# Threshold attention and a relu-squared MLP on one core: the first batch in two sweeps, MLP work in smaller pieces at an even rate, a float64 rounding in three VectorE passes, squares on GpSimd

## The chip, the core and the metric

The kernel runs on one core of a Trainium2 chip. A core has five engines that run side by side, each through its own queue in order: PE (TensorE, matrix products and transposes, results in PSUM), DVE (VectorE), ACT (ScalarE), POOL (GpSimd) and SP (SyncE, which here issues nearly all DMAs). PE loads a stationary operand (PEld in the profile) while it streams an earlier one. On this kernel an fp32 product shows as two matmul instructions, a transpose as one. The metric is the time of one execution on the device in microseconds, less being better.

## What is computed

Two blocks follow each other. The attention has 8 batches of 8 heads, 576 tokens, 64 columns a head:

```python
scores = scale * np.matmul(q, k.transpose(0, 1, 3, 2))          # scale = 1/8
thresh = np.max(scores, axis=-1, keepdims=True) - tau
scores = np.where(scores >= thresh, scores, -1000000000.0)
scores = scores - np.max(scores, axis=-1, keepdims=True)
attn = np.exp(scores)
attn = attn / (np.sum(attn, axis=-1, keepdims=True) + 1e-09)
return np.matmul(attn, v)
```

Its result, as x of 4608 tokens by 512 columns, goes through an MLP with 2048 hidden columns:

```python
h = x @ w_in
r = np.maximum(h, 0.0)
g = r * r
return g @ w_out
```

q, k and v are float32. w_in and w_out reach the kernel as float64, which it takes as pairs of 32-bit words and turns into float32 itself.

## The kernel before

**Attention steps.** Heads are taken in pairs, 4 pairs a batch, 32 in all. A pair has 5 steps: step `i` of 0 to 3 handles 128 query rows of both heads; step 4 handles the last 64 rows of both heads together, with `qmid`, in which the two heads' rows lie block by block. There are 160 steps `s`, 20 for a batch. `scores(g, i)` puts the scores into the PSUM tile `sc` (L167; one buffer of four banks), takes the row maximum on DVE (L172), small values beside it (L173 to L178), the exponential on ACT (L182), the threshold mask with the row sum on DVE (L183), a reciprocal (L186), and the normalisation on POOL (L188). The next `scores` waits until L183 has read `sc`.

`turn(g, i, part)` transposes those weights on PE one step later, in three parts of three 128x128 tiles (L200), each copied to `wT` by ACT (L201) out of one PSUM buffer, tag `tr`. `mix(g, half)` multiplies `wT` with `v` (L227) for 288 of a pair's 576 tokens, twice a pair, and ACT copies the result to `xT` (L230).

**MLP.** Tokens go in 12 chunks of 384. `mlp_in(j, f)` is one of 16 tiles of hidden columns: four products into `h` (L239), relu on ACT (L242), and on DVE the product of `h` and the relu, which is the square (L244). `mlp_out(j, x)` is a quarter of one 128-token output tile, four products (L255); after the fourth, a copy on ACT (L259) and a DMA (L261). Tiles `h` and `o` share two PSUM buffers, tag `mm`.

**Order.** PE runs the written order (`manual_schedule`). The queues of the other engines are ordered by the scheduler of the framework, which can put an instruction ahead of ones that were written earlier. `fill(share)` stands after each part of `turn` and at the end of a step and takes MLP work from a list: `add_chunks` adds the chunks whose tokens are complete, at step 1 of the first pair of the next batch, and `fill` spreads what is there over the rest of that batch. A batch has 576 tokens and a chunk 384, so batches 1 to 7 work on one chunk and two chunks in turn; two chunks remain after the last step.

**Loads.** `load_qk` loads q and k of a pair in 8 DMAs and is written two pairs ahead; `prep` transposes them in 32x32 blocks on DVE (L143), with small copies on POOL (L146, L150). `load_v` loads v in 4 DMAs into one of two tiles. `load_weights` and `round_weights` treat w_in and w_out in 32 pieces of 128x512, two pieces a step, over steps 0 to 17. The raw words lie in an area that is later the second `xT` buffer, with space for two pieces and their scratch. A piece passes DVE (L103), POOL (L104), ACT (L106), DVE (L107, L109, L110), POOL (L111) and DVE (L112).

Of the kernel before, what the change touches and what calls it, by code (L numbers as in the profile page):

```python
# [9 lines left out]
FP32 = mybir.dt.float32  # L10
# [7 lines left out]
def kernel(  # L18
# [66 lines left out]

    def weight_area(i):
        if not area:
            area["a"] = pool.tile([P, NMC, 2 * S], FP32, tag="xT", name="area").rearrange("p c s -> p (c s)")
        at = (i % 2) * 4 * WP
        return (area["a"][:, at:at + 2 * WP], area["a"][:, at + 2 * WP:at + 3 * WP],  # L90
                area["a"][:, at + 3 * WP:at + 4 * WP])

    def load_weights(i):
        nc.sync.dma_start(out=weight_area(i)[0].bitcast(mybir.dt.int64), in_=weight_piece(i)[0])

    def round_weights(i):


        src, p, f = weight_area(i)
        words = src.bitcast(U32).rearrange("p (n w) -> p n w", w=2)  # L100
        lo, hi = words[:, :, 0], words[:, :, 1]
        pu, fu, dst = p.bitcast(U32), f.bitcast(U32), weight_piece(i)[1]
        nc.vector.tensor_scalar(out=fu, in0=hi, scalar1=0x7FF00000, scalar2=None, op0=ALU.bitwise_and)  # L103
        nc.gpsimd.tensor_scalar(out=p, in0=fu, scalar1=float(1151 << 20), scalar2=float(896 << 20),  # L104
                                op0=ALU.min, op1=ALU.max)
        nc.scalar.activation(out=pu, in_=p, func=AF.Copy, bias=-float(896 << 23), scale=8.0)  # L106
        nc.vector.tensor_scalar(out=fu, in0=hi, scalar1=3, scalar2=0x007FFFFF,  # L107
                                op0=ALU.logical_shift_left, op1=ALU.bitwise_and)
        nc.vector.tensor_tensor(out=fu, in0=fu, in1=pu, op=ALU.bitwise_or)  # L109
        nc.vector.scalar_tensor_tensor(out=p, in0=lo, scalar=2.0 ** -52, in1=p, op0=ALU.mult, op1=ALU.mult)  # L110
        nc.gpsimd.tensor_tensor(out=f, in0=f, in1=p, op=ALU.add)  # L111
        nc.vector.scalar_tensor_tensor(out=dst.bitcast(U32), in0=hi, scalar=0x80000000, in1=fu,  # L112
                                       op0=ALU.bitwise_and, op1=ALU.bitwise_or)
# [3 lines left out]
    def load_qk(g):  # L117

        b, h = g // HP, 2 * (g % HP)
        tiles = []  # L120
        for name, t in (("ql", q), ("kl", k)):
            x = pool.tile([P, S // 32, 32], FP32, tag=name, name=name)
            for n in range(4):
                src = t[b, h + n // 2, :, (n % 2) * 32:(n % 2) * 32 + 32]
                nc.sync.dma_start(out=x[n * 32:(n + 1) * 32, :, :], in_=src.rearrange("(c p) d -> p c d", p=32))
            tiles.append(x)
        loaded[g] = tiles

    def load_v(g):
        b, h = g // HP, 2 * (g % HP)  # L130
        t = vs[g % 2]
        for u in range(2):
            at = u * (NBLK + 1)
            nc.sync.dma_start(out=t[:, at:at + NBLK, :],
                              in_=v[b, h + u, 0:NBLK * P, :].rearrange("(c p) d -> p c d", p=P))
            nc.sync.dma_start(out=t[u * D:(u + 1) * D, at + NBLK, :], in_=v[b, h + u, NBLK * P:S, :])

    def prep(g, part):

        if part == 0:  # L140
            ready[g] = [pool.tile([P, S], FP32, tag="qT", name="qT"), pool.tile([P, REST + S], FP32, tag="kT", name="kT")]
        qT, kT = ready[g]
        nc.vector.transpose((qT, kT[:, REST:])[part], loaded[g][part].rearrange("p c d -> p (c d)"))  # L143
        if part == 1:

            nc.gpsimd.tensor_copy(out=kT[D:P, 0:REST], in_=kT[D:P, S:S + REST])  # L146
        else:
            for u in range(2):
                rows = slice(u * D, (u + 1) * D)
                nc.gpsimd.tensor_copy(out=qmid[g % 2][rows, u * D:(u + 1) * D], in_=qT[rows, NBLK * P:S])  # L150
# [3 lines left out]
    def scores(g, i):  # L154


        qT, kT = ready[g]
        n = 2 if i < NBLK else 1
        sc = psum.tile([P, 2 * n, 512], FP32, tag="sc", name="sc")
        for half in range(2):  # L160
            for u in range(n):
                if i < NBLK:
                    rows, lhsT = slice(u * D, (u + 1) * D), qT[u * D:(u + 1) * D, i * P:(i + 1) * P]
                else:
                    rows, lhsT = slice(0, P), qmid[g % 2]
                at = (0 if u else REST) + half * HALF
                nc.tensor.matmul(sc[:, 2 * u + half, 0:HALF], lhsT, kT[rows, at:at + HALF],  # L167
                                 start=True, stop=True)
# [21 lines left out]
        weights[g, i] = w  # L190

    def turn(g, i, part):

        w = weights[g, i]
        ps = psum.tile([P, 4, P], FP32, tag="tr", name="w_ps")
# [21 lines left out]
    def mix(g, half):  # L217

        b, pr = g // HP, g % HP
        if b // 2 not in xTs:  # L220
            xTs[b // 2] = pool.tile([P, NMC, 2 * S], FP32, tag="xT", name="xT")
        cols = slice(half * HALF, (half + 1) * HALF)
        ps = psum.tile([P, HALF], FP32, tag="x", name="x_ps")
        for c in range(NBLK + 1):
            for u in range(2):
                cw = NBLK if c == NBLK else u * (NBLK + 1) + c
                nc.tensor.matmul(ps[u * D:(u + 1) * D, :], vs[g % 2][:, u * (NBLK + 1) + c, :], wT[:, cw, cols],  # L227
                                 start=(c == 0), stop=(c == NBLK))
        to = (b % 2) * S + half * HALF
        nc.scalar.copy(xTs[b // 2][:, pr, to:to + HALF], ps)  # L230
# [3 lines left out]
    def mlp_in(j, f):  # L234

        xT, at = xTs[j * TCH // (2 * S)], j * TCH % (2 * S)
        h = psum.tile([P, TCH], FP32, tag="mm", name="h", bufs=2)
        for c in range(NMC):
            nc.tensor.matmul(h, w_in_sb[:, c, f * P:(f + 1) * P], xT[:, c, at:at + TCH],  # L239
                             start=(c == 0), stop=(c == NMC - 1))  # L240
        r = pool.tile([P, TCH], FP32, tag="r", name="r")
        nc.scalar.activation(out=r, in_=h, func=AF.Relu)  # L242
        gs[j, f] = pool.tile([P, TCH], FP32, tag="g", name="g", bufs=17)
        nc.vector.tensor_tensor(out=gs[j, f], in0=h, in1=r, op=ALU.mult)  # L244

    OQ = 4

    def mlp_out(j, x):

        t, part = divmod(x, OQ)  # L250
# [3 lines left out]
        for f in range(part * NFT // OQ, (part + 1) * NFT // OQ):  # L254
            nc.tensor.matmul(o, gs[j, f][:, t * P:(t + 1) * P], w_out_sb[:, f, :],  # L255
                             start=(f == 0), stop=(f == NFT - 1))
        if part == OQ - 1:
# [5 lines left out]
    waiting = deque()  # L263
    state = {"chunk": 0, "left": 0.0}

    def add_chunks(tokens):
        while state["chunk"] < NCH and (state["chunk"] + 1) * TCH <= tokens:
            j = state["chunk"]
            waiting.extend((3.0, mlp_in, j, f) for f in range(NFT))
            waiting.extend((4.0, mlp_out, j, x) for x in range(TCH // P * OQ))  # L270
            state["chunk"] += 1

    def fill(share):


        total = sum(x[0] for x in waiting)
        state["left"] = min(state["left"] + (total / share if share else 1e9), total)
        while waiting and state["left"] >= waiting[0][0]:
            cost, fn, j, x = waiting.popleft()
            state["left"] -= cost  # L280
            fn(j, x)

    load_qk(0)
    load_v(0)
    load_qk(1)
    for part in range(2):
        prep(0, part)
    NST = NBLK + 1
    steps = [(g, i) for g in range(NPAIR) for i in range(NST)]
    per_batch = HP * NST  # L290
    for s in range(len(steps) + 2):
        g, i = divmod(s, NST)
        shares = 4 * (per_batch - s % per_batch)
        if s < len(steps):
            if i == 0 and 0 < g < NPAIR - 1:
                load_qk(g + 1)
            scores(g, i)
        if i == 1 and g > 0:
            mix(g - 1, 1)
            if g % HP == 0:  # L300
                add_chunks((g // HP) * S)
        for part in range(3):
            if 0 < s <= len(steps):
                turn(*steps[s - 1], part)
            fill(shares - part)
        if s < len(steps):
            if i == 4:
                mix(g, 0)
            if i == 2 and g + 1 < NPAIR:
                load_v(g + 1)  # L310
            if i in (2, 3) and g + 1 < NPAIR:
                prep(g + 1, i - 2)
            if s < n_pieces // 2 + 2:
                for x in (0, 1):
                    if s >= 1 and 2 * s - 2 + x < n_pieces:
                        round_weights(2 * s - 2 + x)
                    if 2 * s + x < n_pieces:
                        load_weights(2 * s + x)
        fill(shares - 3)
    fill(0)  # L320


# [30 lines left out]
```

## Time and profile before

| | us |
|---|---|
| median of 3 runs | 1853.54 |
| lowest and highest run | 1852.3, 1853.58 |
| the profiled execution | 1854.62 |
| its span, first to last instruction | 1852.9 |
| PE busy in the span | 1602.0 |
| DVE busy | 789.2 |
| ACT busy | 570.2 |
| POOL busy | 366.7 |
| mean granted PE clock | 0.95 |

A row of groups reads: line, engine, operation, output<-input, shapes, count, busy us in all and mean ns of one, then the idle time of the engine just before these instructions and what ended it. A row of the timeline reads: start, duration, engine, line, operation, and in brackets the idle time before it. A row by windows gives the stretch and its length, then the busy time of PE, PE's weight loads, DVE, ACT and POOL in it with counts, the granted PE clock as a share of full speed, the DMA share and GB/s. A row of waits gives who waited for whom, us in all, how often, and the longest.

### The profile page before, as it was taken

The numbers are of one execution on the slowest core, as the hardware profiler recorded it, in microseconds if no ns is written. First come the engines' busy times: TensorE is split into PE (matmuls) and PEld (weight loads), VectorE is DVE, ScalarE is ACT, GpSimd is POOL, SyncE is SP. The second block draws the span as 40 slices with busy tenths as digits, with TensorE's granted clock in tenths as the row PEclk, the third lists the DMA queues.
The fourth block names the chain that finished last, engine by engine and source line by source line (L and its number), as shares of the span: only waits on it lengthen the run. The fifth ranks groups of instructions, "written<-read, shape, count | busy, mean of one in ns | idle before, by whom it ended". The sixth has DMA issues, their size and how long they took to land.

```text
span 1852.9 us, 18593 instructions
## 1 busy us (share of the span) xinstructions
PE 1602.0 (86%) x6464; PEld 858.0 (46%) x6464; DVE 789.2 (43%) x1953; ACT 570.2 (31%) x1125; POOL 366.7 (20%) x619
## 2 busy tenths in 40 slices
PE   3455479888999989888999989898999989889999
PEld 2222245445555445445545445444545445445454
DVE  5767845444334345434334335434334335441010
ACT  2333233333323233333223234333223234332010
POOL 4555522111111112111111112221111111120000
PEclk9665589999999999999999999999999999999999
DMA  4433211110010111111011101111011010000000
GB/s 95 118 93 102 85 21 25 26 31 14 18 32 13 24 25 20 29 24 23 13 30 20 25 19 26 21 30 23 16 30 20 16 28 7 7 12 6 12 6 17
DMA packets 200382, 55.74 MB, mean 30 GB/s; under 512 B 191584, under 2 KB 191584, under 8 KB 200288
## 3 DMA queue, kind: packets, MB, share of 16 engines
q1 hardware_dynamic: 200256, 54.55, 13.0%
q8 instruction: 51, 0.84, 0.2%
q14 instruction: 43, 0.35, 0.1%
q0 software_dynamic: 32, 0.00, 0.0%
HBM read 45.09 MB, written 9.44 MB: 29 GB/s over the span
## 4 chain that ended last, share of the span: by engine, by line
PE 76%; DVE 9%; ACT 8%; POOL 4%; issue 3%; DMA 1%; SPq 0%; ACTq 0%; DVEq 0%; POOLq 0%
PE h L239 26%; PE o L255 24%; PE sc L167 9%; PE x_ps L227 9%; PE w_ps L200 8%; ACT w L182 3%; DVE w L183 3%; ACT wT L201 3%; POOL w L188 2%; POOL area L111 1%; DVE st L172 1%; DVE area L109 1%; POOL area L104 1%; PE w_ps L204 1%; DVE area L110 1%
## 5 line engine op out<-in xcount | busy, mean ns | idle before, releaser
L239 PE MATMUL h<-xT,w_in_sb 128*128 128x384 f32 x1536 | 520.9, 487 | 0.0
L255 PE MATMUL o<-w_out_sb,g 128*128 128x512 f32 x1152 | 514.8, 593 | 0.0
L239 PEld LDWEIGHTS h<-xT,w_in_sb 128*128 128x128 f32 x1536 | 280.6, 190 | 171.2 <-issue 6.7
L172 DVE TENSOR_REDUCE st<-sc 128x2 f32<-128x1152 f32 (+1 forms) x160 | 197.8, 1236 | 376.4 <-PE sc L167 372.9
L188 POOL TENSOR_SCALAR w<-w,st 128x576 f32<-128x576 f32 x288 | 242.8, 851 | 466.9 <-DVE st L186 445.4
L200 PE MATMUL w_ps<-ident,w 128*128 128x128 f32 x1152 | 216.6, 300 | 123.0 <-ACT wT L201 105.3
L183 DVE SCALAR_TENSOR_TENSOR w<-sc,st,w 128x576 f32<-128x576 f32 x288 | 235.4, 817 | 184.6 <-ACT w L182 183.0
L255 PEld LDWEIGHTS o<-w_out_sb,g 128*128 128x128 f32 x1152 | 209.7, 190 | 222.2 <-issue 221.6
L201 ACT COPY wT<-w_ps 128x384 f32<-128x384 f32 x384 | 183.7, 478 | 364.4 <-PE w_ps L200 361.9
L182 ACT ACTIVATE w<-sc,st 128x576 f32<-128x576 f32 x288 | 213.8, 742 | 233.3 <-DVE st L173 175.4
L244 DVE TENSOR_TENSOR g<-h,r 128x384 f32<-128x384 f32 x192 | 106.9, 557 | 378.2 <-ACT r L242 378.2
L200 PEld LDWEIGHTS w_ps<-ident,w 128*128 128x128 f32 x1152 | 138.5, 148 | 260.6 <-ACT wT L201 141.9
L167 PE MATMUL sc<-kT,qT 64*128 64x288 f32 x1024 | 180.0, 474 | 87.3 <-DVE w L183 78.9
L242 ACT ACTIVATE r<-h 128x384 f32<-128x384 f32 x192 | 94.1, 490 | 306.0 <-PE h L239 306.0
L227 PE MATMUL x_ps<-wT,vs 128*64 128x288 f32 x1280 | 184.8, 439 | 0.0
L167 PEld LDWEIGHTS sc<-kT,qT 64*128 64x128 f32 x1024 | 98.5, 206 | 173.2 <-DVE w L183 86.1
L178 POOL TENSOR_SCALAR st<-st 128x2 f32<-128x2 f32 (+1 forms) x160 | 33.7, 210 | 665.8 <-DVE st L177 567.3
L227 PEld LDWEIGHTS x_ps<-wT,vs 128*64 128x64 f32 x1280 | 92.6, 148 | 89.2 <-issue 42.9
L259 ACT COPY osb<-o 128x512 f32<-128x512 f32 x36 | 21.1, 586 | 142.9 <-PE o L255 133.9
L167 PE MATMUL sc<-kT,qmid 128*128 128x288 f32 x128 | 41.3, 449 | 20.0 <-DVE w L183 20.0
L230 ACT COPY xT<-x_ps 128x288 f32<-128x288 f32 x64 | 25.5, 398 | 96.0 <-PE x_ps L227 96.0
L111 POOL TENSOR_TENSOR area<-area 128x512 f32<-128x512 f32 x32 | 41.4, 1293 | 44.3 <-DVE area L110 30.3
(39 smaller groups left out, 503.7 us busy)
## 6 DMA issues: line engine op xcount, KB each, us to landing
ql<-in_q_dram SPq DMA_DIRECT2D x128, 72.0 KB, 2.4
kl<-in_k_dram SPq DMA_DIRECT2D x128, 72.0 KB, 2.4
out_dram<-osb SPq DMA_DIRECT2D x36, 256.0 KB, 2.0
vs<-in_v_dram SPq DMA_DIRECT2D x64, 128.0 KB, 2.3
area<-in_moe_w_in_dram SPq DMA_DIRECT2D x16, 512.0 KB, 4.3
area<-in_moe_w_out_dram SPq DMA_DIRECT2D x16, 512.0 KB, 3.6
vs<-in_v_dram SPq DMA_DIRECT2D x64, 16.0 KB, 2.1
ntau<-in_tau_dram POOLq DMA_DIRECT2D x1, 0.5 KB, 3.2
```

The source lines that it names most:

```text
L167: nc.tensor.matmul(sc[:, 2 * u + half, 0:HALF], lhsT, kT[rows, at:at + HALF], start=True, stop=True)
L172: nc.vector.tensor_reduce(out=mx, in_=s, axis=AX.XY, op=ALU.max)
L182: nc.scalar.activation(out=wu, in_=s[:, u], func=AF.Exp, bias=bias[:, u:u + 1], scale=SCALE)
L183: nc.vector.scalar_tensor_tensor(out=wu, in0=s[:, u], scalar=thr[:, u:u + 1], in1=wu, op0=ALU.is_ge, op1=ALU.mult, accum_out=sm[:, u:u + 1])
L188: nc.gpsimd.tensor_scalar(out=w[:, u, :], in0=w[:, u, :], scalar1=z[:, u:u + 1], scalar2=rcp[:, u:u + 1], op0=ALU.add, op1=ALU.mult)
L200: nc.tensor.transpose(ps[:, n, :], w.rearrange("p u k -> p (u k)")[:, c * P:(c + 1) * P], ident)
L201: nc.scalar.copy(wT[:, 3 * part:3 * part + 3, cols], ps[:, 0:3, :])
L227: nc.tensor.matmul(ps[u * D:(u + 1) * D, :], vs[g % 2][:, u * (NBLK + 1) + c, :], wT[:, cw, cols], start=(c == 0), stop=(c == NBLK))
L239: nc.tensor.matmul(h, w_in_sb[:, c, f * P:(f + 1) * P], xT[:, c, at:at + TCH], start=(c == 0), stop=(c == NMC - 1))
L242: nc.scalar.activation(out=r, in_=h, func=AF.Relu)
L244: nc.vector.tensor_tensor(out=gs[j, f], in0=h, in1=r, op=ALU.mult)
L255: nc.tensor.matmul(o, gs[j, f][:, t * P:(t + 1) * P], w_out_sb[:, f, :], start=(f == 0), stop=(f == NFT - 1))
```

## The change

The order of the first batch: `visits` lists, for the four pairs of batch 0, the first three steps of each pair, then the last two of each; from batch 1 on a visit is a pair with its five steps. Each visit loads q, k and v and calls `prep`, so batch 0 has eight such loads instead of four. `mix` takes a range of columns, 0 to 384 and 384 to 576, two steps after the last step that it needs. A chunk is listed at the step where its tokens are complete, which is 13 for chunk 0.

The rate: `rate(s)` is the smallest, over the later releases, of the work that is there up to that release divided by the steps to it. A quarter of it is spent before and after each part of `turn`. A part is half an `mlp_in` or an eighth of an output tile. In steps before the first release, parts 1 and 2 of `turn` use the `mm` buffers.

The rounding: three DVE passes, three on POOL and two on ACT a piece, with scratch tiles of their own (two buffers) and four raw areas; one piece a step in steps 0 to 11, then three. The square is r * r on POOL instead of h * r on DVE. `load_qk` and `prep` come one visit ahead.

```diff
+    RAW = 4
     def weight_area(i):
...
-        at = (i % 2) * 4 * WP
-        return (area["a"][:, at:at + 2 * WP], area["a"][:, at + 2 * WP:at + 3 * WP],
-                area["a"][:, at + 3 * WP:at + 4 * WP])
+        at = (i % RAW) * 2 * WP
+        return area["a"][:, at:at + 2 * WP]
...
-        nc.vector.tensor_scalar(out=fu, in0=hi, scalar1=0x7FF00000, scalar2=None, op0=ALU.bitwise_and)
-        nc.gpsimd.tensor_scalar(out=p, in0=fu, scalar1=float(1151 << 20), scalar2=float(896 << 20),
-                                op0=ALU.min, op1=ALU.max)
-        nc.scalar.activation(out=pu, in_=p, func=AF.Copy, bias=-float(896 << 23), scale=8.0)
-        nc.vector.tensor_scalar(out=fu, in0=hi, scalar1=3, scalar2=0x007FFFFF,
-                                op0=ALU.logical_shift_left, op1=ALU.bitwise_and)
-        nc.vector.tensor_tensor(out=fu, in0=fu, in1=pu, op=ALU.bitwise_or)
-        nc.vector.scalar_tensor_tensor(out=p, in0=lo, scalar=2.0 ** -52, in1=p, op0=ALU.mult, op1=ALU.mult)
-        nc.gpsimd.tensor_tensor(out=f, in0=f, in1=p, op=ALU.add)
-        nc.vector.scalar_tensor_tensor(out=dst.bitcast(U32), in0=hi, scalar=0x80000000, in1=fu,
-                                       op0=ALU.bitwise_and, op1=ALU.bitwise_or)
+        sc = pool.tile([P, 3, WP], FP32, tag="cv", name="cv")
+        t, e, d = sc[:, 0, :], sc[:, 1, :], sc[:, 2, :]
+        tu, eu = t.bitcast(U32), e.bitcast(U32)
+        nc.scalar.activation(out=e, in_=hi.bitcast(FP32), func=AF.Square)
+        nc.gpsimd.tensor_scalar(out=t, in0=e, scalar1=2.0 ** -30, scalar2=2.0 - 2.0 ** -23,
+                                op0=ALU.is_ge, op1=ALU.mult)
+        nc.scalar.activation(out=d, in_=lo, func=AF.Copy, scale=2.0 ** -52)
+        nc.vector.scalar_tensor_tensor(out=tu, in0=hi, scalar=3, in1=tu, op0=ALU.logical_shift_left,
+                                       op1=ALU.bitwise_and)
+        nc.vector.scalar_tensor_tensor(out=tu, in0=hi, scalar=0xC0000000, in1=tu, op0=ALU.bitwise_and,
+                                       op1=ALU.bitwise_or)
+        nc.vector.tensor_scalar(out=eu, in0=tu, scalar1=0xFF800000, scalar2=None, op0=ALU.bitwise_and)
+        nc.gpsimd.tensor_tensor(out=d, in0=d, in1=e, op=ALU.mult)
+        nc.gpsimd.tensor_tensor(out=dst, in0=t, in1=d, op=ALU.add)
...
+        tag = "mm" if early() and part else "tr"
+        ps = psum.tile([P, 4, P], FP32, tag=tag, name="w_ps", bufs=2 if tag == "mm" else 1)
...
-        for c in range(NMC):
+        for c in range(part * NMC // 2, (part + 1) * NMC // 2):
...
-        nc.vector.tensor_tensor(out=gs[j, f], in0=h, in1=r, op=ALU.mult)
+            nc.gpsimd.tensor_tensor(out=gs[j, f], in0=r, in1=r, op=ALU.mult)
...
+    FIRST = TCH // P
+    visits = [(g, list(range(FIRST))) for g in range(HP)] + [(g, list(range(FIRST, NBLK + 1))) for g in range(HP)]
+    visits += [(g, list(range(NBLK + 1))) for g in range(HP, NPAIR)]
+    steps = [(n, i) for n in range(len(visits)) for i in visits[n][1]]
...
+        if i in (FIRST - 1, NBLK):
+            cols = slice(0, TCH) if i < NBLK else slice(TCH, S)
+            mixes[s + 2] = (n, cols)
+            g = visits[n][0]
+            if g % HP == HP - 1:
+                complete[s + 2] = g // HP * S + cols.stop
...
+    IN_US, OUT_US = 1.28, 0.427 * 2 * OF
+    CHUNK_US = NFT * (2 * IN_US + TCH // P * OUT_US / OF)
...
+    def early():
+        return state["step"] < min(chunk_at)
...
+    def rate(s):
+        have = sum(x[0] for x in waiting)
+        best = 1e9
+        for e in sorted(chunk_at) + [NST + 2]:
+            if e > s:
+                best = min(best, have / (e - s))
+                have += CHUNK_US * len(chunk_at.get(e, ()))
+        return best
+    def fill(us):
+        state["left"] += us
+        while waiting and state["left"] >= waiting[0][0] / 2:
+            cost, fn, *what = waiting.popleft()
             state["left"] -= cost
-            fn(j, x)
+            fn(*what)
+    pieces = [1 if s < min(chunk_at) - 1 else 3 for s in range(NST)]
...
+    for s in range(NST + 3):
+        state["step"] = s
+        if s < NST:
+            n, i = steps[s]
+            if i == visits[n][1][0] and n + 1 < len(visits):
+                load_qk(n + 1)
+            scores(n, i)
+        if s in mixes:
+            mix(*mixes[s])
+        for j in chunk_at.get(s, ()):
+            add_chunk(j)
+        quarter = rate(s) / 4 if s < NST + 2 else 1e9
+        fill(quarter)
         for part in range(3):
...
+            fill(quarter)
+        if s < NST:
+            at = visits[n][1].index(i)
+            if n + 1 < len(visits):
+                if at == 1:
+                    prep(n + 1, 0)
+                    prep(n + 1, 1)
+                if at == len(visits[n][1]) - 1:
+                    load_v(n + 1)
+            for i in range(done, min(done + pieces[s], n_pieces)):
+                if i + RAW - 1 < n_pieces:
+                    load_weights(i + RAW - 1)
+                round_weights(i)
+                done += 1
```

150 lines of the change are left out of this document (63 added, 87 removed).

## Prediction

> **What bounds the kernel now.** The page comes first: shares of busy time, the forty slices, then the groups.
>
> ```profile
> span 1852.9 us, 18593 instructions
> PE 1602.0 (86%) x6464; PEld 858.0 (46%) x6464; DVE 789.2 (43%) x1953; ACT 570.2 (31%) x1125; POOL 366.7 (20%) x619
> PE   3455479888999989888999989898999989889999
> PEclk9665589999999999999999999999999999999999
> ```
>
> PE is the only engine near full, but not everywhere: five poor slices at a granted clock of 0.5 to 0.6, then stretches of 8 between stretches of 9. The table by windows, cut where the row maximum (L172) of steps 0, 20, 40 and 60 starts, and at the tail, says why.
>
> ```profile
> core 0: us, PE busy (x) PEld busy (x) DVE busy (x) ACT busy (x) POOL busy (x), PEclk, DMA share, GB/s
> 11.10:240.50 229.40, 111.91 (x447) 59.53 (x448) 164.97 (x363) 73.59 (x136) 113.72 (x135) 0.67 0.37 95
> 240.50:418.10 177.60, 154.47 (x697) 83.39 (x698) 82.73 (x216) 64.30 (x127) 35.80 (x68) 0.99 0.13 25
> 418.10:662.10 244.00, 234.51 (x921) 125.86 (x922) 92.02 (x233) 73.00 (x146) 35.85 (x68) 0.99 0.10 21
> ...
> 1680.00:1852.90 172.90, 168.18 (x471) 86.55 (x470) 17.85 (x32) 20.69 (x43) 0.00 (x0) 1.00 0.03 10
> ...
> L172 DVE TENSOR_REDUCE st<-sc x65: 745/1357/1360, 11.1 to 697.3; 128x2 f32<-128x1152 f32 x52, 128x1 f32<-128x576 f32 x13
> ```
>
> Four regimes. Batch 0 (229.4 us, 20 steps) has no MLP chunk, and DVE and POOL round the weights. A batch with one chunk (177.6) leaves PE idle for 177.60 - 154.47 = 23.1 us. A batch with two (244.0) leaves it idle for 9.5. The tail holds two chunks alone. So PE bounds the two-chunk batches and the tail, the attention chain shares the one-chunk batches, and batch 0 belongs to DVE and POOL.
>
> Price of a chunk, from the tail's timeline: the first h matmul, and the copy after the last o matmul.
>
> ```profile
> 1683.74 16.71 PE L239 MATMUL h<-xT,w_in_sb 128*128 128x384 f32 x51
> ...
> 1849.05 0.59 ACT L259 COPY osb<-o 128x512 f32<-128x512 f32 x1 [13.19 <-PE o L255]
> ```
>
> 1849.05 - 1683.74 = 165.3 for two, **82.65 us a chunk**. Dense attention then costs PE 244.0 - 165.3 - 9.5 = 69.2 us a batch, **3.46 us a step**.
>
> What PE waits for (us in all, times, longest), two rows of the one-chunk batch and the first of the two-chunk batch:
>
> ```profile
> PE w_ps L200 <- ACT wT L201: 13.4, 21, 1.3
> ...
> PE w_ps L200 <- POOL w L188: 1.0, 3, 0.5
> ...
> PE w_ps L200 <- ACT wT L201: 4.9, 7, 1.3
> ```
>
> The largest share is transposes that follow each other with no MLP matmul between them: one PSUM buffer, so the next group waits for ACT's copy, 0.6 to 0.7 us each time.
>
> **The change, part by part.** The time is summed stage by stage along PE, as each stage ends where its last PE work does.
>
> *Two sweeps and the even rate.* By the new planner's arithmetic chunk 0 is released at step 13 instead of 21, and chunks 1 to 11 at 39, 41, 59, 79, 81, 99, 119, 121, 139, 159, 161. The rate is the smallest slope to any later release: 3.15 us a step from 13 to 38 (chunk 0 over 26 steps), then 6.1 to 6.2 a step from 39 to 158 (nine chunks over 120), where before 4.1 and 8.2 took turns. Two chunks stay for the tail, as before.
>
> Steps 39 to 158: each has 9 x 82.65 / 120 = 6.20 us of MLP and 3.46 of attention. The smaller parts (1.28 and 1.71 us) put one into nearly every quarter of a step; of the 468 quarters of steps 41 to 157 my count leaves 23 empty, each worth a wait of 0.7 (4.9/7 above): 16 us over 117 steps, 0.14 a step. Sum 9.80 x 120 = 1176. Bounds: no wait at all, 1159; the idle of the two-chunk batch, 0.475 a step, 1216.
>
> Steps 20 to 38: PE has 3.15 + 3.46 = 6.6 us a step, about the attention chain's own pace, which two successive reductions with little filler show:
>
> ```profile
> 301.81 1.36 DVE L172 TENSOR_REDUCE st<-sc 128x2 f32<-128x1152 f32 x1
> ...
> 308.35 1.36 DVE L172 TENSOR_REDUCE st<-sc 128x2 f32<-128x1152 f32 x1 [0.61 <-PE sc L167]
> ...
> 470.92 2.65 PE L227 MATMUL x_ps<-wT,vs 128*64 128x288 f32 x20
> ```
>
> 6.5 us. The mixes lie unevenly on that: one of 288 columns is 2.65 us (last row), so 384 columns cost 3.5 and 192 cost 1.8. Without a mix PE needs 6.6 less 5.3/5, so 5.5, and the chain's pace holds, taken as 6.7; with the large mix PE needs 9.0, with the small one 7.3. Three fifths at 6.7, one at 9.0 and one at 7.3 (taken as 7.5, as it is near the chain): 7.3 mean, 19 x 7.3 = 139. Bounds 126 (PE alone) and 168 (8.87, the one-chunk batch's step).
>
> *Steps 0 to 19: rounding.* The rows of its passes, and those of the neighbours that price the new ones:
>
> ```profile
> L103 DVE TENSOR_SCALAR area<-area 128x512 uint32<-128x512 uint32 x32 | 13.4, 420 | 3.1 <-DMA area<-in_moe_w_out_dram 1.7 <-DMA area<-in_moe_w_in_dram 1.4
> L104 POOL TENSOR_SCALAR area<-area 128x512 f32<-128x512 uint32 x32 | 22.3, 697 | 34.8 <-DVE area L103 10.4 <-DVE st L173 9.8 <-DVE st L185 7.4
> L106 ACT ACTIVATE area<-area 128x512 uint32<-128x512 f32 x32 | 20.2, 630 | 58.4 <-POOL area L104 58.4
> L107 DVE TENSOR_SCALAR area<-area 128x512 uint32<-128x512 uint32 x32 | 13.6, 425 | 13.7 <-POOL area L104 13.4
> L109 DVE TENSOR_TENSOR area<-area 128x512 uint32<-128x512 uint32 x32 | 23.8, 743 | 5.0 <-ACT area L106 4.8
> L110 DVE SCALAR_TENSOR_TENSOR area<-area 128x512 f32<-128x512 uint32 x32 | 22.8, 711 | 0.4
> L111 POOL TENSOR_TENSOR area<-area 128x512 f32<-128x512 f32 x32 | 41.4, 1293 | 44.3 <-DVE area L110 30.3 <-DVE st L185 5.7 <-DVE st L177 5.0
> L112 DVE SCALAR_TENSOR_TENSOR w_out_sb<-area 128x512 uint32<-128x512 uint32 x16 | 11.5, 717 | 12.7 <-POOL area L111 12.5
> L112 DVE SCALAR_TENSOR_TENSOR w_in_sb<-area 128x512 uint32<-128x512 uint32 x16 | 11.1, 691 | 10.8 <-POOL area L111 10.6
> L143 DVE STREAM_TRANSPOSE qT<-ql 128x576 f32<-128x576 f32 x32 | 24.6, 769 | 1.0 <-DMA ql<-in_q_dram 1.0
> ```
>
> A piece on DVE: 0.42 + 0.425 + 0.743 + 0.711 + 0.70 = 3.0 us before; two passes like L110 and one like L103, 1.84, after: 32 x 1.16 = 37 us less. On POOL: 0.70 + 1.29 = 1.99 before, one like L104 and two like L111, 3.28, after: 41 us more. On ACT one pass more, 0.63 (20 us, at 73.59 of 229.40 busy it has room). Four extra visits add 4 x 2 transposes of 0.77 on DVE (6 us), four small copies on POOL and 48 DMA issues on SP. load_qk moves from two visits ahead to one, behind up to three weight loads on SP's queue; if those hold it, the first step of a visit waits. Such a load lands in
>
> ```profile
> area<-in_moe_w_in_dram SPq DMA_DIRECT2D x16, 512.0 KB, 4.3
> ```
>
> 4.3 us, so at most that for 8 visits, 34. I price it at nothing, because four raw areas let the loads be issued early.
>
> So DVE falls and POOL rises by the same amount. Whether that counts depends on whether the two can work at once. The timeline has POOL's L104 twice, alone and beside a DVE pass with two SBUF operands:
>
> ```profile
> 138.44 0.61 POOL L104 TENSOR_SCALAR area<-area 128x512 f32<-128x512 uint32 x1 [2.49 <-DVE st L173]
> ...
> 141.11 0.69 DVE L110 SCALAR_TENSOR_TENSOR area<-area 128x512 f32<-128x512 uint32 x1
> 141.35 0.92 POOL L104 TENSOR_SCALAR area<-area 128x512 f32<-128x512 uint32 x1 [1.78 <-DVE area L103]
> ```
>
> 0.92 beside L110 against 0.61. The times of a piece on the two therefore add: 4.99 before, 5.12 after. I leave **229.4 us** for the first 20 steps. Bounds: -25, if the waits that the shorter chain removes (L107 behind L104 13.4, L112 behind L111 23.1, most of it) all come off the path; +36, if POOL's 41 us more lie on it, less what DVE frees.
>
> The Trainium skill, "SBUF — State Buffer", section "Who interferes with whom", says that DVE and GpSimd hold one port pair as an exclusive lock, against a DVE instruction with two SBUF inputs too. By that rule moving passes to GpSimd shortens nothing, which is a sum of 229 here; without it DVE's 37 us less would count and give about 192. The two L104 rows agree with the rule.
>
> During steps 13 to 19 the planner lays 17 parts, 22 us of chunk 0, beside this: that is the gain of the two sweeps, and it is already in the 139 above; PE was busy for only 111.91 of 229.40. The second buffers for early transposes remove waits there (L200 on L201), but the next scores wait later still, for L183: nothing.
>
> *Squares on POOL.*
>
> ```profile
> L188 POOL TENSOR_SCALAR w<-w,st 128x576 f32<-128x576 f32 x288 | 242.8, 851 | 466.9 <-DVE st L186 445.4 <-PE h L239 10.6 <-PE w_ps L200 10.0
> L244 DVE TENSOR_TENSOR g<-h,r 128x384 f32<-128x384 f32 x192 | 106.9, 557 | 378.2 <-ACT r L242 378.2
> L242 ACT ACTIVATE r<-h 128x384 f32<-128x384 f32 x192 | 94.1, 490 | 306.0 <-PE h L239 306.0
> ```
>
> DVE loses 192 x 0.557 (L244). POOL gains 192 passes of 128x384 with two inputs: between 0.57 (L188 scaled, one input) and 1.29 (L111, wider); I take 0.97, L111 scaled by width. PE takes 2.58 us a tile (82.65/32), so POOL has time; the last g of a chunk is read only by the eighth output part, 7 x 1.71 = 12 us later. Cost nothing; if the cover fails, see the third rival.
>
> *Ends.*
>
> ```profile
> 1670.68 0.76 DVE L172 TENSOR_REDUCE st<-sc 128x1 f32<-128x576 f32 x1 [4.77 <-PE sc L167]
> ...
> 1673.27 3.60 PE L255 MATMUL o<-w_out_sb,g 128*128 128x512 f32 x8
> ```
>
> Start to first reduction 11.1; from step 159's reduction to the end 1852.9 - 1670.7, less 3.6 of an old chunk and 0.6 of waits that the two new chunks cover, 178.
>
> **Sum:** 11.1 + 229.4 + 139 + 1176 + 178 = 1733.5 span. The profiled run took 1854.62 for a span of 1852.9, and the median of the runs is 1.1 less than it: **1734 us**.
>
> **The rivals.** *First: POOL bounds the start.* For it: POOL and DVE exclude each other, and three pieces a step in steps 12 to 18 are 15 us of both, beside 1.7 of L188. Against: 164.97 + 113.72 is 49 us more than the 229.40 of batch 0, so they do overlap beside other passes (L172, L183). Steps 0 to 19 take 265: 1770. *Second: the start shrinks.* Three hand-overs a piece instead of five, loads four deep: 204, so 1709. *Third, the slower end:* POOL's queue is in order; if a square that waits for relu stands ahead of the normalisation (L188), the transposes, and PE with them, wait for relu 0.49, square 0.97, normalisation 0.82 and hand-overs, 2.6 us. It decides from 119 / 2.6 = 46 of the 146 steps with squares or outputs; if half of them are hit, 190 us, 1924. Against: PE's waits for L188 are 1.0 us in the one-chunk batch. The Trainium skill, "GPSIMD Engine Reference", section "Engine selection", advises VectorE for elementwise work, GpSimd being about twice as slow with two inputs; L111 against L244 per column is 1.7. *Fourth: the even rate leaves the idle that the two-chunk batch has:* 1774. *Fifth: the change doesn't do what it says.* Only PE keeps the written order; the other queues are ordered by the scheduler, so one and three pieces a step may not come out so. That moves time within the first two.
>
> **How the numbers follow.** Forecast 0.36; first rival 0.22; second 0.20; third 0.05; fourth 0.15; other 0.02. The forecast, both start cases and the fourth lie between 1690 and 1800; outside lie the third and the ends of sums, about 0.2. About 0.2% is what a measurement here can tell from no change. Faster is all but the third and half of the others: 0.94; slower is the third, 0.05; same 0.01.
>
> **What would show it.** Step 20's reduction near 240 us; steps 20 to 38 at 7.3; 39 to 158 at 9.8 with PE idle under 0.3 a step; L200's waits on L201 well under the 13.4 us of one one-chunk batch in any 20 steps; the square near 0.97 on POOL; a tail of 165. It is wrong if batch 0 stays low in PE past 270 us, or if transposes wait for POOL in the dense part.

## The result and the profile after

The changed kernel takes 1757.8 us (median of 4 runs, 1756.38 to 1758.94) against 1853.56 for the kernel before: a ratio of 0.9485, 95% interval 0.9468 to 0.9501. The forecast was 1734 with a range of 1690 to 1800. The profiled execution has a span of 1756.3 us, 96.6 less than before.

The page of the changed kernel: span, shares, and the slices of PE and its clock.

```profile
span 1756.3 us, 18657 instructions
PE 1570.3 (89%) x6464; PEld 847.3 (48%) x6464; DVE 693.0 (39%) x1705; ACT 575.4 (33%) x1157; POOL 610.1 (35%) x847
PE   2443648888999999999999999999999999999999
PEclk9566788999999999999999999999999999999999
```

From the eleventh slice on PE is full without a break: the stretches of 8 between stretches of 9 are gone. The start is not better: six slices at 2 to 6, where before there were five and a 7. POOL went from 366.7 us busy to 610.1.

The table by windows of the changed kernel, cut at the row maxima of steps 0, 20, 39 and 159 (columns as before: length, PE, PEld, DVE, ACT, POOL, clock, DMA).

```profile
core 0: us, PE busy (x) PEld busy (x) DVE busy (x) ACT busy (x) POOL busy (x), PEclk, DMA share, GB/s
11.20:283.50 272.30, 125.62 (x515) 72.97 (x515) 158.53 (x305) 92.56 (x175) 206.87 (x178) 0.73 0.36 88
283.50:432.60 149.10, 129.22 (x593) 68.47 (x595) 74.40 (x193) 56.45 (x114) 40.26 (x73) 0.97 0.18 34
432.60:1580.40 1147.80, 1140.70 (x4850) 615.23 (x4852) 456.01 (x1198) 402.21 (x819) 332.36 (x551) 1.00 0.11 23
1580.40:1756.30 175.90, 172.07 (x503) 88.87 (x501) 2.30 (x8) 22.90 (x48) 27.44 (x34) 1.00 0.03 11
```

The stages, from the starts of the same row maxima in every run (a step is the mean of its stage; the time is the median of three or four executions for before, after, e1 and e12, and one execution for the others; those of the changed kernel lie within 2.6 us of each other):

| run | steps 0-19, us | a step of 20-38 | a step of 39-158 | time, us |
|---|---|---|---|---|
| before | 229.4 | 8.83 | 10.52 | 1853.5 |
| forecast | 229.4 | 7.3 | 9.80 | 1734 |
| after | 272.3 | 7.85 | 9.565 | 1757.8 |
| e1_min | 271.2 | 7.85 | 9.564 | 1757.7 |
| e2_sq_dve | 266.4 | 7.89 | 9.559 | 1752.4 |
| e3_old_round | 230.8 | 7.79 | 9.565 | 1717.1 |
| e4_no_round | 156.9 | 7.73 | 9.565 | 1640.7 |
| e5_one_sweep | 269.2 | 7.86 | 9.583 | 1757.5 |
| e6_coarse | 277.9 | 7.98 | 10.312 | 1855.9 |
| e7_batch_rate | 275.4 | 7.89 | 9.806 | 1800.5 |
| e8_flat2 | 267.2 | 7.75 | 9.565 | 1751.2 |
| e9_u32 | 272.9 | 7.86 | 9.565 | 1758.9 |
| e10_coarse_x | 276.2 | 7.51 | 9.673 | 1768.6 |
| e11_minmax | 238.3 | 7.78 | 9.565 | 1723.0 |
| e12_best | 221.9 | 7.24 | 9.484 | 1686.8 |

So the change lost 43 us in the first 20 steps and won 19 in steps 20 to 38 (167.8 to 149.1), 115 in steps 39 to 158 (1262.4 to 1147.7) and some 6 at the end.

Steps 39 to 158 of the kernel before by windows, and the two largest waits of PE in them:

```profile
408.30:1670.70 1262.40, 1165.49 (x4850) 627.10 (x4849) 522.51 (x1342) 411.60 (x819) 214.29 (x405) 0.99 0.10 21
...
PE w_ps L200 <- ACT wT L201: 54.3, 84, 1.3
...
PE sc L167 <- DVE w L183: 30.4, 17, 3.8
```

With two smaller kinds, of 9.2 and 3.0 us, the waits of PE are 97 us. In the changed kernel, the same steps:

```profile
PE w_ps L207 <- ACT wT L208: 6.2, 9, 1.2
```

That is the whole list: nine waits in 120 steps. (L207 and L208 are the transposes and copies, L200 and L201 before.) So 91 of the 115 us are waits that are gone. The rest shows as a shorter busy time of PE for as many matmul instructions (4850, in 1165.5 and 1140.7 us); where that time was lost is not shown. In steps 0 to 19 of the changed kernel, the largest wait of PE and the largest of DVE:

```profile
PE sc L173 <- DVE w L189: 103.4, 15, 13.0
...
DVE cv L111 <- POOL cv L108: 76.7, 30, 6.6
```

The scores wait for the mask of the step before (L189), which stands in DVE's queue behind a rounding pass (L111), which waits for POOL's threshold pass (L108). Its group, and those of the other passes:

```profile
L256 POOL TENSOR_TENSOR g<-r 128x384 f32<-128x384 f32 x192 | 160.1, 834 | 351.6 <-ACT r L254 348.9 <-ACT wT L219 1.9
...
L108 POOL TENSOR_SCALAR cv<-cv 128x512 f32<-128x512 f32 x32 | 65.0, 2031 | 14.8 <-ACT cv L107 12.8
L116 POOL TENSOR_TENSOR cv<-cv 128x512 f32<-128x512 f32 x32 | 45.4, 1419 | 17.1 <-DVE st L191 6.2 <-DVE cv L115 3.4 <-DVE st L183 3.2
...
L113 DVE SCALAR_TENSOR_TENSOR cv<-area,cv 128x512 uint32<-128x512 uint32 x32 | 29.7, 928 | 0.2
...
L117 POOL TENSOR_TENSOR w_out_sb<-cv 128x512 f32<-128x512 f32 x16 | 23.2, 1452 | 0.9
L111 DVE SCALAR_TENSOR_TENSOR cv<-area,cv 128x512 uint32<-128x512 uint32 x32 | 22.7, 710 | 76.7 <-POOL cv L108 76.7
L117 POOL TENSOR_TENSOR w_in_sb<-cv 128x512 f32<-128x512 f32 x16 | 22.5, 1405 | 1.3
L115 DVE TENSOR_SCALAR cv<-cv 128x512 uint32<-128x512 uint32 x32 | 21.9, 684 | 0.5
```

L108 takes 2.03 us where the forecast had 0.70. POOL's work a piece is 2.03 + 1.42 + 1.43 = 4.88 us, not 3.28, and 32 of them are 156 of its 207 us in the stage.

### The profile page after: what moved, and what is told of

Its sections match the earlier page's. It is cut to its first block, busy times and chain, and to the rows that moved or that the text cites. A ratio compares the mean times of both kernels' runs of the same rounds, so it can differ in the third digit from the quotient of the medians.

```text
span 1756.3 us, 18657 instructions
## 1 busy us (share of the span) xinstructions
PE 1570.3 (89%) x6464; PEld 847.3 (48%) x6464; DVE 693.0 (39%) x1705; ACT 575.4 (33%) x1157; POOL 610.1 (35%) x847
## 4 chain that ended last, share of the span: by engine, by line
PE 79%; POOL 4%; ACT 3%; DVE 3%; issue 1%; ACTq 0%; DVEq 0%; POOLq 0%
PE o L266 27%; PE h L250 27%; PE sc L173 9%; PE x_ps L234 8%; PE w_ps L207 6%; POOL cv L108 2%; ACT w L188 2%; DVE st L178 1%; POOL w_out_sb L117 1%; DVE w L189 1%; POOL cv L116 1%; ACT wT L208 1%; POOL w L194 1%; PE w_ps L211 0%; ACT wT L214 0%
## 5 line engine op out<-in xcount | busy, mean ns | idle before, releaser
L250 PE MATMUL h<-xT,w_in_sb 128*128 128x384 f32 x1536 | 551.9, 494 | 0.0
L266 PE MATMUL o<-w_out_sb,g 128*128 128x512 f32 x1152 | 539.6, 598 | 0.0
L194 POOL TENSOR_SCALAR w<-w,st 128x576 f32<-128x576 f32 x288 | 237.7, 834 | 317.3 <-DVE st L192 296.5
L189 DVE SCALAR_TENSOR_TENSOR w<-sc,st,w 128x576 f32<-128x576 f32 x288 | 235.3, 817 | 198.9 <-ACT w L188 197.9
L266 PEld LDWEIGHTS o<-w_out_sb,g 128*128 128x128 f32 x1152 | 200.6, 190 | 189.0 <-issue 187.7
L256 POOL TENSOR_TENSOR g<-r 128x384 f32<-128x384 f32 x192 | 160.1, 834 | 351.6 <-ACT r L254 348.9
L208 ACT COPY wT<-w_ps 128x384 f32<-128x384 f32 x384 | 182.4, 477 | 278.6 <-PE w_ps L207 278.2
L173 PE MATMUL sc<-kT,qT 64*128 64x288 f32 x1024 | 175.7, 460 | 97.6 <-DVE w L189 82.1
L207 PEld LDWEIGHTS w_ps<-ident,w 128*128 128x128 f32 x1152 | 150.5, 146 | 195.7 <-issue 100.1
L207 PE MATMUL w_ps<-ident,w 128*128 128x128 f32 x1152 | 196.9, 286 | 43.1 <-ACT wT L208 25.5
L173 PEld LDWEIGHTS sc<-kT,qT 64*128 64x128 f32 x1024 | 97.4, 200 | 183.7 <-issue 136.9
L234 PE MATMUL x_ps<-wT,vs 128*64 128x192 f32 (+1 forms) x1280 | 178.4, 427 | 0.0
L108 POOL TENSOR_SCALAR cv<-cv 128x512 f32<-128x512 f32 x32 | 65.0, 2031 | 14.8 <-ACT cv L107 12.8
L173 PE MATMUL sc<-kT,qmid 128*128 128x288 f32 x128 | 40.6, 443 | 29.9 <-DVE w L189 29.9
L111 DVE SCALAR_TENSOR_TENSOR cv<-area,cv 128x512 uint32<-128x512 uint32 x32 | 22.7, 710 | 76.7 <-POOL cv L108 76.7
L116 POOL TENSOR_TENSOR cv<-cv 128x512 f32<-128x512 f32 x32 | 45.4, 1419 | 17.1 <-DVE st L191 6.2
```

Source lines behind the costliest of these rows:

```text
L108: nc.gpsimd.tensor_scalar(out=t, in0=e, scalar1=2.0 ** -30, scalar2=2.0 - 2.0 ** -23, op0=ALU.is_ge, op1=ALU.mult)
L189: nc.vector.scalar_tensor_tensor(out=wu, in0=s[:, u], scalar=thr[:, u:u + 1], in1=wu, op0=ALU.is_ge, op1=ALU.mult, accum_out=sm[:, u:u + 1])
L194: nc.gpsimd.tensor_scalar(out=w[:, u, :], in0=w[:, u, :], scalar1=z[:, u:u + 1], scalar2=rcp[:, u:u + 1], op0=ALU.add, op1=ALU.mult)
L207: nc.tensor.transpose(ps[:, n, :], w.rearrange("p u k -> p (u k)")[:, c * P:(c + 1) * P], ident)
L208: nc.scalar.copy(wT[:, 3 * part:3 * part + 3, cols], ps[:, 0:3, :])
L234: nc.tensor.matmul(ps[u * D:(u + 1) * D, 0:nq], vs[n % 2][:, u * (NBLK + 1) + c, :], wT[:, cw, cols], start=(c == 0), stop=(c == NBLK))
```

## Experiments

Theory: the first 20 steps are set by the rounding on POOL and DVE, above all by POOL's passes, and the steady part by whether MLP work lies between the transposes. Rivals: the eight visits with later loads, and the order of the pieces, make the start long; the even rate alone, or the squares' move, makes the steady part.

### The rounding

**e3_old_round**: the old rounding, scratch and areas as in the changed kernel.

```diff
-        (2 ACT, 3 DVE and 3 POOL passes of the change)
+        (L103 to L112 of before, with p and f in a tile "cv")
```

> The rounding of before (five DVE passes, two on POOL, one on ACT) in the changed loop, with the four raw areas and two scratch buffers. Theory POOL: POOL does 1.99 us a piece instead of 4.9, DVE 3.0 instead of 2.3, their sum is as before: steps 0 to 19 take 225 to 240, the run 1712 to 1725, so the new rounding costs the change 35 to 45 us. Rival order: steps 0 to 19 stay above 262.

Measured: 1717.1, steps 0 to 19 in 230.8. The stage by windows, with POOL at 130 us instead of 207 and DVE at 173 instead of 159:

```profile
12.70:243.50 230.80, 123.43 (x515) 71.11 (x515) 172.65 (x368) 74.16 (x143) 130.24 (x146) 0.74 0.43 101
```

As the theory said. The visits and loads of the two sweeps are in this kernel too, so they don't make the start long. The new rounding costs the change 41 us.

**e4_no_round**: the rounding left out.

```diff
-        (the passes of the change)
+        nc.scalar.activation(out=dst, in_=hi.bitcast(FP32), func=AF.Copy)
```

> The rounding is left out: one ACT copy of each high word takes its place, so the weights are not the reference's. Both theories: this shows what the start costs without DVE and POOL passes. At the bare pace of an attention step at low clock, 8.2 us, with the mixes on top: steps 0 to 19 take 165 to 180. Theory POOL: steps 20 to 38 stay near 7.85. If they fall to 7.3, rounding reaches into them.

Measured: 156.9 for the first 20 steps, under the expected 165 to 180, and 7.73 a step after them. The rounding is worth 115 us of the 272.3, and it hardly reaches past step 20.

**e1_min, e9_u32, e11_minmax**: three forms of the threshold pass.

```diff
 e1_min
-scalar1=2.0 ** -30, scalar2=2.0 - 2.0 ** -23, op0=ALU.is_ge, op1=ALU.mult
+scalar1=2.0 ** 31, scalar2=2.0 - 2.0 ** -23, op0=ALU.mult, op1=ALU.min
 e9_u32
-in0=e, scalar1=2.0 ** -30
+in0=eu, scalar1=float(97 << 23)
 e11_minmax
-func=AF.Square)
+func=AF.Square, scale=2.0 ** 16)
-scalar1=2.0 ** -30, scalar2=2.0 - 2.0 ** -23, op0=ALU.is_ge, op1=ALU.mult
+scalar1=2.0 - 2.0 ** -23, scalar2=0.0, op0=ALU.min, op1=ALU.max
```

> The threshold pass of the rounding on POOL (L108) does a multiplication and a minimum instead of a comparison and a multiplication; its result is the same for every weight whose float32 value is normal or zero. Theory POOL: the start is set by POOL's work a piece, 2.03 + 1.42 + 1.43 = 4.9 us. L108 falls from 2.03 to about 0.65, steps 0 to 19 from 272 to 235 (230 to 245), the run to 1720. Rival order: the start is long because of eight visits with later loads, and because of hand-overs between engines; then L108 gets shorter and steps 0 to 19 stay above 262, the run above 1747.

The group of L108 in that run:

```profile
L108 POOL TENSOR_SCALAR cv<-cv 128x512 f32<-128x512 f32 x32 | 64.9, 2029 | 13.8 <-ACT cv L107 11.8
```

The pass got no shorter, so the run tells nothing between the theories: the ratio to before is 0.9485 (0.9469 to 0.95), that of the change. The pass is as slow without a comparison. Next, the input's type:

> The threshold pass on POOL reads the same squares as uint32 words (a comparison with the bit pattern of the threshold, the same result), as L104 of before read uint32. If the float32 input is what made it 2.03 us against 0.70: L108 falls to 0.6 to 0.8, and by theory POOL (43 us of POOL work less) steps 0 to 19 fall from 272 to 232 to 250 and the run to 1720 to 1737. If the input's type has no part in it, L108 stays at 2.0 and the run within 4 us of 1758.

```profile
L108 POOL TENSOR_SCALAR cv<-cv 128x512 f32<-128x512 uint32 x32 | 65.2, 2037 | 14.8 <-ACT cv L107 12.8
```

Not the type either. Last, the pair of operations that L104 had:

> The threshold pass is a minimum and a maximum, the pair of operations of L104 of before; ACT's square is scaled by 2 to the 32 so that the result is the same for normal and zero weights. If the pair of operations is what makes L108 2.03 us: it falls to 0.6 to 0.75, and by theory POOL (43 us of POOL less) steps 0 to 19 fall from 272 to 230 to 250 and the run to 1716 to 1737. If L108 gets short and steps 0 to 19 stay over 262, theory POOL falls. If L108 stays at 2.0, its cause stays open.

The group of L108, then the stage by windows:

```profile
L108 POOL TENSOR_SCALAR cv<-cv 128x512 f32<-128x512 f32 x32 | 21.8, 682 | 18.0 <-ACT cv L107 17.6
```

```profile
11.20:249.00 237.80, 121.96 (x514) 71.56 (x514) 161.81 (x304) 92.78 (x175) 158.61 (x178) 0.79 0.41 101
```

0.68 us with a minimum and a maximum, and the first 20 steps fall by 34 us to 238.3, the run to 1723.0. POOL lost 32 x 1.35 = 43 us of work and the path 34. Both slow pairs hold a multiplication by a constant, but why they are slow stays open: the normalisation (L194, an addition and a multiplication with one scalar a partition) takes 0.834 us for 576 columns. This run also scales the squares that the pass reads, so the pair of operations is not quite the only difference.

**e8_flat2**: the order of the pieces.

```diff
-    pieces = [1 if s < min(chunk_at) - 1 else 3 for s in range(NST)]
+    pieces = [2 for s in range(NST)]
```

> Two pieces a step in steps 0 to 15 instead of one and then three. Theory POOL: the order written for the pieces changes nothing, as POOL's work a piece sets the pace: steps 0 to 19 within 6 us of 272. Rival order: three pieces a step make the long steps, and steps 0 to 19 fall below 255.

Measured 267.2, 5 us less, and 1751.2 in all. The written order sets little; the timeline of the changed kernel shows why. Here are L108 and the scores in step 0, for which one piece is written:

```profile
13.98 1.94 POOL L108 TENSOR_SCALAR cv<-cv 128x512 f32<-128x512 f32 x1 [5.18 <-ACT cv L107]
...
16.77 1.92 POOL L108 TENSOR_SCALAR cv<-cv 128x512 f32<-128x512 f32 x1
...
20.31 2.29 PE L173 MATMUL sc<-kT,qT 64*128 64x288 f32 x8 [9.16 <-DVE w L189]
```

Two pieces are begun before the second scores: the scheduler pulls later pieces ahead of what was written before them. The third has to wait until a scratch tile is free, as there are two. What ACT's first pass of a piece (L107) waits for in these 20 steps, where L117 is the last pass of an earlier piece:

```profile
ACT cv L107 <- POOL w_in_sb L117: 33.2, 5, 9.5
...
ACT cv L107 <- POOL w_out_sb L117: 26.0, 10, 5.6
```

Whether more scratch tiles would shorten the start was not tried.

### The two sweeps

**e5_one_sweep**:

```diff
-    visits = (HP pairs with steps 0 to 2, then the same with steps 3 and 4, then the rest)
+    visits = [(g, list(range(NBLK + 1))) for g in range(NPAIR)]
```

> Batch 0 goes pair by pair again, in one sweep; all else as changed, so chunk 0 is released at step 19 and spread to step 39. If the two sweeps pay by the MLP work that they put beside the start (some 22 us of chunk 0 in steps 13 to 19): steps 0 to 19 get 5 to 10 us shorter (four visits fewer), steps 20 to 38 rise from 7.85 to about 8.7 each, and the run is 1760 to 1772. If the PE time of the first sweep is worth nothing, it is 1758 or less.

Measured 1757.5, the time of the change; the start is 3 us shorter, less than the expected 5 to 10. Chunk 0 is then spread over steps 19 to 39, 4.1 us a step instead of 3.15, and these steps still take 7.86. In the changed kernel PE is idle for 149.10 - 129.22 = 20 us of them, and that room holds the additional work: PE is busy for 141.2 us there in this run. So with this rounding the first sweep's early chunk buys nothing that a run here can tell.

### The steady part

**e6_coarse**: large parts at the even rate.

```diff
-    (half an mlp_in, 1.28 us; OF = 2)
+    (a whole mlp_in, 2.56 us; OF = 4)
```

> The MLP parts are as large as before (a whole mlp_in, a quarter of an output tile) at the even rate. If the smaller parts are what removes the transposes' waits for ACT's copies: the waits of L207 on L208 rise from 6 to 40 us and more in steps 39 to 158, a step from 9.56 to 9.9, the run to about 1800. If the even rate alone does it: below 9.65 a step, 1758 to 1770.

Measured 1855.9, more than the expected 1800, with 10.31 us a step. That is the time of the kernel before, but with a start 48 us longer than there; in steps 39 to 158 it still gains 25 us on it (10.52 a step). PE's waits in these steps:

```profile
PE w_ps L207 <- ACT wT L208: 65.9, 91, 1.4
PE w_ps L217 <- ACT wT L214: 10.4, 8, 1.4
PE sc L173 <- DVE w L189: 2.4, 4, 0.8
```

Together 78.7 us, 72.5 more than in the changed kernel; the stage lost 90. A part of 2.6 or 3.4 us at 1.54 us a quarter leaves about every other quarter empty, and there the next transposes wait for ACT to empty the one buffer. The direct test of that is another buffer, with the large parts kept:

**e10_coarse_x**:

```diff
+        if tag == "tr" and part == 1 and i < NBLK:
+            ps = psum.tile([P, TCH], FP32, tag="x", name="w_ps").rearrange("p (c k) -> p c k", k=P)
```

> Large MLP parts as in the earlier coarse run, but the middle part of each turn uses the buffer of the mixes (tag x), so that two transposes in a row no longer share one. If the coarse run lost its 90 us because one buffer makes the transposes wait where no MLP work lies between them: steps 39 to 158 fall from 10.31 to below 9.75 each and the run to 1775 to 1790. If large parts cost by themselves, by holding up the scores: above 10.1, over 1825.

Measured 1768.6, 6 us below the range expected, and 9.673 a step. The waits (the transposes are L210 here, their copies L211; L220 is the pair of transposes in step 4 that has no such buffer, L240 the copy of a mix):

```profile
PE w_ps L220 <- ACT wT L217: 10.4, 8, 1.4
PE w_ps L210 <- ACT wT L211: 6.2, 8, 1.0
PE sc L173 <- DVE w L189: 3.6, 5, 1.0
PE w_ps L210 <- ACT xT L240: 2.3, 5, 0.5
```

65.9 fell to 6.2 + 2.3. Large parts cost mainly by the shared buffer, not by themselves: of the 13 us that are left against the change, 10.4 are the waits in step 4 (L220), which has no second buffer. The smaller parts of the change and a second buffer are two remedies for one wait.

**e7_batch_rate**: small parts at the rate of before.

```diff
+    (chunks 1 to 11 released at steps 41, 61, 81 and so on)
-            if e > s: best = min(best, have / (e - s))
+            if e > s: return have / (e - s)
```

> Small parts, but the rate of before: chunks 1 to 11 are released at the batch boundaries (41, 61, 81 and so on) and each spread to the next boundary, so that one and two chunks a batch take turns. If the even rate is what pays: batches with one chunk fall back to some 8 us a step with PE waiting for attention, 10 to 14 us in each of four, the run 1795 to 1810. If the small parts alone do it: 1758 to 1770.

Measured 1800.5: 29 us more in steps 39 to 158 and 9 in the tail. The even rate is worth 43 us beside small parts. PE's waits in steps 39 to 158 are 32 us here (20.6 for ACT's copies, 10.9 for the mask, 0.8 in step 4) against 6.2.

**e2_sq_dve**: the squares back on DVE.

```diff
-            nc.gpsimd.tensor_tensor(out=gs[j, f], in0=r, in1=r, op=ALU.mult)
+            nc.vector.tensor_tensor(out=gs[j, f], in0=h, in1=r, op=ALU.mult)
```

> The square goes back to DVE (h times relu), all else as changed. Theory POOL: only some 7 squares fall into steps 0 to 19, so the start gets 5 to 10 us shorter, and steps 39 to 158 stay at 9.56 each within 0.1, as PE bounds them: 1748 to 1762. Rival squares: the squares delay the normalisation, and steps 20 to 38 go from 7.85 to 7.3 and the run below 1745.

Measured 1752.4: 6 us less in the first 20 steps, where POOL does the rounding too, and 9.559 against 9.565 a step later. The move to POOL is neutral where PE bounds and a small loss at the start.

### A faster version

**e12_best**: the edits of e2, e8, e11 and of e10's buffer (with small parts), and one more:

```diff
-        nc.scalar.activation(out=d, in_=lo, func=AF.Copy, scale=2.0 ** -52)
-        nc.gpsimd.tensor_tensor(out=d, in0=d, in1=e, op=ALU.mult)
+        nc.vector.scalar_tensor_tensor(out=d, in0=lo, scalar=2.0 ** -52, in1=e, op0=ALU.mult, op1=ALU.mult)
```

> Put together what the runs showed to help: the minimum and maximum in L108, the low word times the exponent in one DVE pass instead of an ACT copy and a POOL product, squares on DVE, two pieces a step, the middle part of each turn in the buffer of the mixes. POOL then has 0.61 + 1.26 a piece, DVE 0.69 + 0.69 + 0.42 + 0.69, 4.4 us together against 4.9 in the run with minimum and maximum: 32 x 0.57 = 18 us less on the two. If the start follows the sum of both engines' passes: steps 0 to 19 at 210 to 225, the run 1690 to 1708. If it follows POOL's own work alone, which is then less than with the old rounding's loop beside it, and DVE becomes the bound: steps 0 to 19 at 226 to 240, the run 1709 to 1722.

Measured 1686.8 (1686.4 to 1686.94), ratio to before 0.9104 (0.9088 to 0.9119), faster than both kernels. The first 20 steps by windows:

```profile
11.20:233.00 221.80, 116.95 (x515) 68.35 (x515) 170.46 (x344) 74.61 (x143) 115.06 (x138) 0.71 0.45 107
```

221.9 us, in the range expected if the sum of both engines' passes counts: DVE grew from 162 to 170 us against e11 and POOL fell from 159 to 115, and the stage got shorter by 16. Since three other edits are in it, this does not separate their shares. The run is faster than the expected 1690, as the later steps got shorter too: 7.24 and 9.484, with no wait of PE left in steps 39 to 158.

## Why the prediction came out as it did

The direction and the range held; the forecast was 23 us too low by the spans (1733.5 and 1756.3), the sum of four differences: 43 us too low for steps 0 to 19, 10 too low for steps 20 to 38, 28 too high for steps 39 to 158 and 2 too high for the end. That the total came so near is in part luck, as errors of both signs met. One of the prediction's own signs of being wrong did appear: PE stays low past 270 us, and step 20's reduction starts at 283.5 us instead of near 240.

*Steps 0 to 19: 229.4 forecast, 272.3 measured.* The step that failed is "one like L104 and two like L111, 3.28": the threshold pass was priced by a neighbour with the same shape and instruction but another pair of operations. It is 2.03 us, not 0.70, and POOL rose by 93 us (113.7 to 206.9) instead of 41; 43 of the 52 more are that pass. e11 takes the pass back to 0.68, and the stage comes to 238.3, near the 229.4. The rival "POOL bounds the start" had this outcome (265), by its own mechanism, with a chance of 0.22.

*Loads.* "load_qk moves from two visits ahead to one" and "written two pairs ahead" in the description of the kernel before are wrong: both kernels write the loads of the next pair at the first step of the present one. Only the second pair's loads moved, from ahead of step 0 into it. So the 34 us that the forecast put at nothing were hardly at risk; PE's waits for transposed keys (L173 on L149 and L152) are 4.7 and 2.2 us in the first 20 steps.

*The times of DVE and POOL add.* For single passes this held, and it shows more plainly in the changed kernel. Five rows of its timeline: POOL's product and DVE's pass each with nothing of the other engine beside it, then DVE's L111, POOL's sum and DVE's L113 as they overlap.

```profile
25.28 1.26 POOL L116 TENSOR_TENSOR cv<-cv 128x512 f32<-128x512 f32 x1
...
82.52 0.68 DVE L113 SCALAR_TENSOR_TENSOR cv<-area,cv 128x512 uint32<-128x512 uint32 x1
...
28.59 0.69 DVE L111 SCALAR_TENSOR_TENSOR cv<-area,cv 128x512 uint32<-128x512 uint32 x1 [6.01 <-POOL cv L108]
28.63 1.77 POOL L117 TENSOR_TENSOR w_in_sb<-cv 128x512 f32<-128x512 f32 x1
29.31 1.63 DVE L113 SCALAR_TENSOR_TENSOR cv<-area,cv 128x512 uint32<-128x512 uint32 x1
```

The sum begins 0.04 us after L111 does and takes 1.77 us where the product, a pass of the same shape, takes 1.26 alone. L113 begins inside the sum, takes 1.63 us instead of 0.68 and ends 0.54 after it. In these rows the pass that begins later is held up. The Trainium skill, "SBUF — State Buffer", section "Who interferes with whom", calls this an exclusive lock between DVE passes with two SBUF inputs and GpSimd passes that read SBUF; these rows agree, but those of the slow threshold pass do not all, as told at the end.

So moving work from DVE to POOL shortened nothing here. With the threshold pass short (e11) the first 20 steps are still 7.5 us longer than with the old rounding (e3), and the slow pass adds the other 34 of the 41 us. That the whole stage follows the sum of both engines is not shown. In e12, e3, e11 and the change the stage grows with that sum (285.5, 302.9, 320.4 and 365.4 us), but POOL's time alone (115, 130, 159 and 207) gives the same order.

*Steps 20 to 38: 7.3 forecast, 7.85 measured.* Mis-sized: the forecast had only the chain and the mixes there. PE's waits for ACT's copies, which it had counted only for the later stage, are there too (L207 on L208, 9.6 us in 14 waits), as parts lie in only two or three of four quarters; with the buffer of e10 the step is 7.51 even with large parts.

*"That is the gain of the two sweeps"* was wrong: e5 has one sweep and takes the same time. What shortened these steps from 8.83 is present with one sweep as well; the parts, the rate and the columns of the mixes are what that run shares with the change, and which of them it is was not separated.

*Steps 39 to 158: 9.80 forecast, 9.565 measured.* The mechanism held: even rate and small parts together end the waits, 6.2 us in 120 steps where 0.14 a step, 17, were foreseen. The rest is the price of attention: 9.565 - 6.20 - 0.05 = 3.31 us a step instead of 3.46. The 3.46 is a difference taken from the kernel before, where PE's busy time for as many matmul instructions is 25 us longer over these steps than after; so it probably held lost time that did not show as idle.

*Squares on POOL: nothing* held: 0.83 us each (0.97 forecast), no wait of PE for POOL in the dense part; 6 us at the start (e2), which the forecast did not count. The rival with the slower end did not occur.

*The fifth rival* was right in part: the written order of the pieces binds little (e8), and it moved 7 us.

*Ends: 178* forecast, 175.9 measured.

One reading of the forecast's was off without any term resting on it: the five poor slices at the start have granted clocks of 0.9, 0.6, 0.6, 0.5 and 0.5, not 0.5 to 0.6 in all.

## What to carry to other kernels

Price a pass by a row with the same pair of operations, not only the same engine, shape and type. Before work is spread more evenly, look at what stands between two uses of a single buffer: with large parts the steady steps went only from 10.52 to 10.31 us, with small ones to 9.57, and sharing the buffer of the mixes brought the large parts to 9.67. Before work is moved between two engines that lengthen each other's passes, price the passes on both: here the move lost 7.5 us even with a short threshold pass.

## What the runs showed of the hardware that was not expected

A POOL pass with two constants over 128x512 took 1.92 us where it ran alone (2.03 in the mean) as a comparison and a multiplication or as a multiplication and a minimum, on float32 or uint32 input, and 0.68 us in the mean as a minimum and a maximum. These forms are not enough to say which operation does it.

The slow pass does not always hold the other engine up. In step 0 of the changed kernel DVE's L113 ran in the middle of L108 (16.77 to 18.69, quoted above) at its usual length:

```profile
17.30 0.69 DVE L113 SCALAR_TENSOR_TENSOR cv<-area,cv 128x512 uint32<-128x512 uint32 x1
```

An exclusive lock held for the whole pass would have kept it until 18.69. This is no single case: of the ten L113 passes that overlap an L108, seven took 0.69 us or less and three 0.98 to 1.12. The other way round the hold shows every time: each of the six L108 passes that begin beside an L111 took 2.42 or 2.43 us against 1.92 alone. Why the slow pass lets most of the DVE passes through stays open.
